# Sliding-window attention followed by a hard-swish MLP on one core: batch 0's values loaded by heads, and batch 1's attention moved against its MLP units

## The chip, the cores and the metric

The kernel runs on one core of a Trainium2 chip. A core has five engines that run their own instruction streams in order and meet at semaphores: TensorE (matmuls and transposes, into PSUM), VectorE, ScalarE, GpSimd (called POOL in the profile) and SyncE (SP), which here only issues DMAs. The metric is device time in microseconds (us), the median of several executions.

## The reference

Inputs are q, k, v of shape (8 batches, 8 heads, 576 tokens, 64), and two weights, w_in (512 x 2048) and w_out (2048 x 512). All are float32.

```python
scores = q @ k.T / 8            # per batch and head
scores = where(0 <= i - j < 128, scores - slope[h] * |i - j|, -1e9)
attn = softmax(scores) @ v      # causal, a window of 128 tokens
x = attn laid out as (8 * 576 tokens, 512)
h = x @ w_in                    # 512 -> 2048
g = h * clip(h + 3, 0, 6) / 6
out = g @ w_out                 # 2048 -> 512, 4608 rows
```

## The kernel before

**Attention, by pairs of heads.** The unit of attention is a pair g = 4b + hp: batch b, heads 2hp and 2hp+1. There are 32 pairs. q and k are cast to bf16 and transposed on TensorE into `qTb` and `kTb` (one copy each for even and odd batches). `double` (line 248) transposes two pairs of one of q and k in two parts through a small PSUM bank, `wide_double` (276) all of it through a wide score buffer. `scores_diag` (313) and `scores_off` (341) make the scores of the diagonal and the off-diagonal blocks in two score buffers of tag "sc", of which there are two in all. `exp_diag` and `exp_off_full` (371, 362) take the exponentials on ScalarE into `pd` and `po`; for batch 1, GpSimd masks the diagonal blocks. `attend` (434) and `attend_split` (444) multiply by the values `vbuf`, which carry a column of ones for the sums, and VectorE divides (a reciprocal and a product) into `avs`. `back` (462) transposes `avs` into `xT`, the MLP's input, five transposes on TensorE and a copy out of PSUM.

**MLP, by tiles and units.** The 4608 rows are cut into nine tiles of 512. A tile has 16 up units (`moe_up`, 508): four matmuls of 128x512 over the model dimension, then ScalarE's relu (516), then VectorE's product (517) into `gbuf`. It has 16 down units (`moe_down`, 534): four matmuls each into one row block of 128. `up_begin` and `up_more` (496, 501) issue some of an up unit's matmuls ahead. `ORDER` (559) is a string of U and D per tile that fixes the order of units; `fill(n)` (569) issues the next n of them, and goes no further than the batches whose attention is finished (`done`).

**PSUM.** Banks are shared by tag: "sc" two wide buffers, "h" two, "av" one, "o" one. An instruction that first writes a bank waits until the last reader of its former contents is done. `UP_BANKS` (506) tells which of the first tile's up units use "av" or "o" instead of "h".

**Order.** The program is scheduled by hand: each engine gets its instructions in the order in which the Python code writes them, and nothing is reordered. `first_batch` (604) and `second_batch` (679) write out batches 0 and 1 and the 16 up units of the first tile; `segment` (743) runs the other pairs in a loop. TensorE, ScalarE, VectorE and GpSimd queues, and the DMA queues of SP, ScalarE and GpSimd, are all in that order.

**Loads.** q and k of batch 0 come first, on SP and ScalarE. v of batch 0 comes as five blocks of 128 tokens by all heads (`load_block`, 108), the first quarter of w_in as float32 into half of `gbuf` (`load_raw`, 176; `cast_raw` casts it), the other three quarters by GpSimd's DMA, which casts on the way (`load_w_in`, 168). The exponentials of batch 0 lie in w_out's buffer and those of batch 1 in the second `gbuf`, so w_out is loaded after batch 0. SP's loads of batch 1 (`load_double`, `load_tokens`) come after `attend(0)` in the code.

Of the lines that the steps below speak of, these say most:

```python
UP_BANKS = {2: "av", 5: "o", 8: "av", 11: "o", 12: "av"}            # line 506
eng = nc.vector.tensor_copy if g == 2 * NP - 1 else nc.scalar.copy   # line 478, the copy of back
```

## Time and profile before

| what | value |
|---|---|
| median of 3 runs | 323.69 us (323.47 to 324.67) |
| span of the profiled execution, first to last instruction | 321.8 us |
| the profiled execution's own time | not listed apart from its span; the median lies 1.9 us above the span |
| TensorE busy | 308.2 us, 96% of the span |
| ScalarE, VectorE, GpSimd busy | 196.0, 175.5, 138.4 us |
| granted TensorE clock | 1.00 throughout |
| DMA read and written | 36.70 and 9.44 MB |

The profile is of one execution. A row of a timeline gives the start, the duration, the engine, the line of the kernel, the operation, what it writes and reads, how many instructions are merged in it, and in brackets the engine's idle time before it and who ended it. A row's duration is from its first start to its last end; back to back, the next one starts a little earlier than that end. A row of windows gives each engine's busy time and, in parentheses, its number of instructions, and then the clock, the share of the DMA engines that were busy, and GB/s.

### The profile page before, as it was taken

Reading aid. Unit: us, or ns where it says so; the run is one execution under the profiler, and the core shown is the slowest. Engines: PE = TensorE matmul, PEld = TensorE weight load, DVE = VectorE, ACT = ScalarE, POOL = GpSimd, SP = SyncE. Lnnn points to the kernel's source line nnn. Section 1 sums busy time; section 2 is a strip of 40 time slices with the busy share of each in tenths; the row PEclk is TensorE's granted clock in tenths of the full one; section 3 lists DMA queues with packets and bytes.
Section 4 is the critical chain, followed back from the end, with each engine's and each line's share of the span. In section 5 each row is a group of like instructions: output and inputs, shape, how many; then the busy total and the mean of one; then the engine's idle time right before and its main releaser. Section 6 shows DMA issues by size and latency. Waiting matters only on the chain.

```text
span 321.8 us, 6865 instructions
## 1 busy us (share of the span) xinstructions
PE 308.2 (96%) x2620; PEld 164.6 (51%) x2659; DVE 175.5 (55%) x346; ACT 196.0 (61%) x337; POOL 138.4 (43%) x247
## 2 busy tenths in 40 slices
PE   6888999999999999999999999999999999999996
PEld 3564465455555545455667655455454444444443
DVE  6686595564346655555555556554655455445510
ACT  3857977877777766766676667666764344244401
POOL 7364590665494767446654663663331000000000
PEclk9999999999999999999999999999999999999999
DMA  7999999899999999999799999922011200000112
GB/s 273 262 369 210 269 233 214 235 200 189 201 256 170 242 200 189 204 202 230 179 214 207 211 189 202 236 66 89 20 55 59 80 34 34 33 33 35 65 49 83
DMA packets 131426, 52.43 MB, mean 163 GB/s; under 512 B 118977, under 2 KB 122817, under 8 KB 131393
## 3 DMA queue, kind: packets, MB, share of 16 engines
q1 hardware_dynamic: 125648, 46.15, 67.0%
q0 software_dynamic: 3696, 3.67, 7.0%
q10 hardware_dynamic: 2048, 2.16, 2.2%
q8 instruction: 21, 0.34, 0.5%
q14 instruction: 13, 0.10, 0.1%
HBM read 36.70 MB, written 9.44 MB: 143 GB/s over the span
## 4 chain that ended last, share of the span: by engine, by line
PE 83%; DMA 7%; ACT 4%; issue 2%; DVE 2%; POOL 1%; SPq 0%; ACTq 0%; DVEq 0%
PE ops L547 37%; PE hps L492 35%; DMA gbuf<-in_moe_w_in_dram 3%; PE scd L324 2%; DMA w_in_sb<-in_moe_w_in_dram 2%; PE av L419 2%; DMA ldbuf<-in_k_dram 2%; PE av L411 2%; ACT r L516 2%; PE sco L356 1%; PE ops L528 1%; DVE gbuf L517 1%; PE tp L254 1%; ACT gbuf L379 1%; ACT xT L479 1%
## 5 line engine op out<-in xcount | busy, mean ns | idle before, releaser
L517 DVE SCALAR_TENSOR_TENSOR gbuf<-r,hps 128x512 bf16<-128x512 f32 x144 | 98.5, 687 | 102.3 <-ACT r L516 99.4
L516 ACT ACTIVATE r<-hps,bias 128x512 f32<-128x512 f32 x144 | 98.8, 690 | 90.4 <-PE hps L492 89.3
L492 PE MATMUL hps<-xT,w_in_sb 128*128 128x512 bf16 (+1 forms) x622 | 143.3, 357 | 2.3 <-DMA w_in_sb<-in_moe_w_in_dram 0.9
L547 PE MATMUL ops<-w_out_sb,gbuf 128*128 128x512 bf16 x539 | 134.0, 379 | 2.4 <-issue 1.7
L492 PEld LDWEIGHTS <-w_in_sb 128*128 128x128 bf16 x640 | 59.0, 98 | 55.3 <-issue 1.7
L547 PEld LDWEIGHTS <-gbuf 128*128 128x128 bf16 x560 | 52.2, 98 | 56.9
L382 POOL TENSOR_SCALAR_AFFINE_SELECT pd<-pd 128x512 bf16<-128x512 bf16 x48 | 29.5, 631 | 37.8 <-ACT pd L379 37.7
L392 POOL TENSOR_SCALAR_AFFINE_SELECT po<-po 128x512 bf16<-128x512 bf16 x48 | 30.1, 633 | 32.6 <-ACT po L389 32.4
L556 DVE COPY osb<-ops 128x512 f32<-128x512 f32 x33 | 22.7, 688 | 22.0 <-PE ops L547 21.9
L379 ACT ACTIVATE pd<-scd,bias_d 128x512 bf16<-128x512 f32 x48 | 31.5, 684 | 4.7 <-PE scd L324 4.7
L389 ACT ACTIVATE po<-sco,bias_o 128x512 bf16<-128x512 f32 x48 | 33.1, 690 | 0.0
L206 POOL CAST tbuf<-ldbuf 128x512 bf16<-128x512 f32 (+1 forms) x45 | 25.5, 611 | 17.1 <-issue 17.1
L430 DVE TENSOR_TENSOR avs<-av,rc 128x384 bf16<-128x384 f32 (+1 forms) x48 | 23.6, 491 | 1.6
L419 PEld LDWEIGHTS <-pd 128*128 128x128 bf16 x192 | 14.3, 97 | 7.9 <-issue 0.5
L411 PE MATMUL av<-vbuf,po 128*128 128x65 bf16 x192 | 18.0, 193 | 0.0
L419 PE MATMUL av<-vbuf,pd 128*128 128x65 bf16 x192 | 17.3, 194 | 0.0
L411 PEld LDWEIGHTS <-po 128*128 128x128 bf16 x192 | 14.3, 98 | 2.9 <-DVE avs L430 0.5
L395 ACT ACTIVATE p4buf<-sco,bias_d 128x64 bf16<-128x64 f32 x48 | 15.6, 325 | 0.0
L199 POOL CAST vbuf<-ldbuf 128x1024 bf16<-128x1024 f32 x14 | 14.2, 1041 | 2.4 <-DMA ldbuf<-in_v_dram 2.4
L324 PEld LDWEIGHTS <-kTb 64*128 64x128 bf16 x256 | 7.3, 94 | 14.3 <-issue 10.0
L324 PE MATMUL scd<-qTb,kTb 64*128 64x128 bf16 x256 | 12.7, 219 | 1.9 <-ACT kTb L232 1.2
L239 POOL CAST pr<-ldbuf 128x576 bf16<-128x576 f32 x18 | 11.5, 671 | 2.0 <-DMA ldbuf<-in_k_dram 1.9
(107 smaller groups left out, 216.7 us busy)
## 6 DMA issues: line engine op xcount, KB each, us to landing
out_dram<-osb SPq DMA_DIRECT2D x33, 256.0 KB, 2.5
ldbuf<-in_v_dram SPq DMA_DIRECT2D x31, 256.0 KB, 5.0
ldbuf<-in_q_dram SPq DMA_DIRECT2D x20, 256.0 KB, 4.8
ldbuf<-in_k_dram SPq DMA_DIRECT2D x16, 256.0 KB, 4.6
ldbuf<-in_q_dram SPq DMA_DIRECT2D x12, 288.0 KB, 6.4
ldbuf<-in_k_dram SPq DMA_DIRECT2D x12, 288.0 KB, 6.7
w_out_sb<-in_moe_w_out_dram POOLq DMA_DIRECT2D x4, 512.0 KB, 10.0
w_in_sb<-in_moe_w_in_dram POOLq DMA_DIRECT2D x3, 512.0 KB, 8.6
```

The lines of the kernel that those rows point to most:

```text
L206: nc.gpsimd.tensor_copy(out=tbuf[:m, :, j, :], in_=s[:m, j, :, :].rearrange("p (i e) d -> p i (e d)", e=2))
L324: nc.tensor.matmul(scd[:, e, ts(j, 128)], lhsT=kT[r, j, :], rhs=qT[r, j, :], start=first, stop=first or j == 3)
L379: nc.scalar.activation(out=pd[:, e, :, :].rearrange("p j c -> p (j c)"), in_=sc[:, e, :], func=ACT.Exp, bias=bias_d[:, h:h + 1], scale=scale)
L382: nc.gpsimd.affine_select(out=pd[:, e, :, :], in_=pd[:, e, :, :], pattern=[[0, 4], [1, 128]], channel_multiplier=-1, base=0, compare_op=AL ...
L389: nc.scalar.activation(out=po[:, e, :, :].rearrange("p j c -> p (j c)"), in_=sc[:, e, :], func=ACT.Exp, bias=bias_o[:, h:h + 1], scale=scale)
L392: nc.gpsimd.affine_select(out=po[:, e, :, :], in_=po[:, e, :, :], pattern=[[0, 4], [-1, 128]], channel_multiplier=1, base=-1, compare_op=A ...
L411: nc.tensor.matmul(out_av, lhsT=po[:, e, qt % 4, :], rhs=vb[:, qt - 1, h, :], start=True, stop=False)
L419: nc.tensor.matmul(out_av, lhsT=d, rhs=vb[:, qt, h, :], start=(qt == 0), stop=True)
L492: nc.tensor.matmul(hps[:, lo:hi], lhsT=w_in_sb[:, ks, ts(ms, 128)], rhs=xT[:, ks, ds(src, hi - lo)], start=(ks == 0), stop=(ks == n_ks - 1))
L516: nc.scalar.activation(out=r6, in_=hps, func=ACT.Relu, bias=bias3[:, 0:1], scale=1.0 / 6.0)
L517: nc.vector.scalar_tensor_tensor(out=gts[nt][:, ms, :], in0=r6, scalar=1.0, in1=hps, op0=ALU.min, op1=ALU.mult)
L547: nc.tensor.matmul(ops[nt, sub], lhsT=gts[nt][:, ms, ts(sub, 128)], rhs=w_out_sb[:, ms, :], start=(ms == 0), stop=(ms == n_ms - 1))
```

## The change

Five things change; no matmul is added or taken away.

- Batch 0's v is loaded by pairs of heads (`load_heads`, the first four token blocks of one head per DMA, and one DMA for the last 64 tokens), all on SP; w_in's first quarter comes in four DMAs between them and is cast on GpSimd alone. `cast_heads` casts v by pairs on GpSimd. Attends 0 and 1 go in between the scores of pairs 2 and 3, and the memsets of `kTb` and `vbuf` for batch 1 stand early now, those of `p4buf` and `tbuf` late.
- SP's loads of batch 1 stand earlier in the code, its v by heads too.
- Up units 0 to 3 are begun before batch 1's first scores, unit 1 in "o" and unit 2 in "av". The wide transposes of batch 1's first half move behind unit 2. The second quarter of w_in is issued between the two halves of batch 1's k cast (`prepare_half`), the third after them.
- In `second_batch`, the transposes of batch 1's second half (now through "av", "o" and "h") and the scores of pairs 4 and 5 come before unit 4; the scores of pairs 6 and 7 among units 4 to 8, and the attends and backs of pairs 4 to 7 among units 8 to 14. Batch 2's double transposes and its first scores come after unit 15. `back` copies with VectorE for all of batch 1.
- The order of the second tile's units begins UUUUD instead of UUDUD.

```diff
--- before.py
+++ after.py
@@ -109,6 +109,12 @@
         n = min(128, S - j * 128)
         eng.dma_start(out=tokens(b, nm)[:n, j, :, :],
                       in_=src_of[nm][b, :, ds(j * 128, n), :].rearrange("h p d -> p h d"))
+
+    def load_heads(b, nm, hp, eng):
+        for e in range(2):
+            h = 2 * hp + e
+            eng.dma_start(out=tokens(b, nm)[:, 0:4, h, :],
+                          in_=src_of[nm][b, h, 0:512, :].rearrange("(j p) d -> p j d", p=128))
 
     def load_tokens(b, nm):
         for j in range(NQ):
@@ -141,12 +147,13 @@
         nc.gpsimd.memset(vbuf[0][:, :, :, D:W], 1.0)
         nc.gpsimd.memset(vbuf[0][64:128, 4, :, 0:D], 0.0)
 
+        nc.gpsimd.memset(kTb[1][:, :, 4, LAST:128], 0.0)
+        nc.gpsimd.memset(vbuf[1][:, :, :, D:W], 1.0)
+        nc.gpsimd.memset(vbuf[1][64:128, 4, :, 0:D], 0.0)
+
     def memsets_later():
         for i in range(2):
             nc.gpsimd.memset(p4buf[i], 1.0)
-        nc.gpsimd.memset(kTb[1][:, :, 4, LAST:128], 0.0)
-        nc.gpsimd.memset(vbuf[1][:, :, :, D:W], 1.0)
-        nc.gpsimd.memset(vbuf[1][64:128, 4, :, 0:D], 0.0)
         nc.gpsimd.memset(tbuf[64:128, :, 4, :], 0.0)
 
     def warm_up(n):
@@ -173,8 +180,8 @@
     raw = gbuf[0][:, n_ms // 2:n_ms, :].rearrange("p m c -> p (m c)").bitcast(FP32).rearrange(
         "p (k f) -> p k f", k=n_ks)
 
-    def load_raw():
-        nc.sync.dma_start(out=raw, in_=moe_w_in[:, 0:512].rearrange("(k p) f -> p k f", p=128))
+    def load_raw(ks):
+        nc.sync.dma_start(out=raw[:, ks, :], in_=moe_w_in[ds(ks * 128, 128), 0:512])
 
     def cast_raw(ks, copy):
         copy(out=w_in_sb[:, ks, 0:512], in_=raw[:, ks, :])
@@ -184,13 +191,12 @@
             out=w_out_sb[:, ts(g, 4), :],
             in_=moe_w_out[ds(g * 512, 512), :].rearrange("(m p) d -> p m d", p=128))
 
-    def second_w_in():
-        nc.gpsimd.memset(w_out_sb[:, 4, 0:1], 0.0)
-        load_w_in(1)
-
     def cast_v(b, j, copy):
         n = min(128, S - j * 128)
         copy(out=vbuf[b % 2][:n, j, :, 0:D], in_=ld[b, "v"][:n, j, :, :])
+
+    def cast_heads(b, hp, copy):
+        copy(out=vbuf[b % 2][:, 0:4, ds(2 * hp, 2), 0:D], in_=ld[b, "v"][:, 0:4, ds(2 * hp, 2), :])
 
     def cast_tokens(b, nm):
         s = ld[b, nm]
@@ -231,6 +237,13 @@
                     nc.tensor.transpose(tp[r, t, :], src[r, ts(t, D)], ident[r, r])
             copy(out=dst[:, hp, :, :].rearrange("p j c -> p (j c)")[:, 0:S].rearrange(
                 "p (a t) -> p a t", t=RT), in_=tp.rearrange("p t a -> p a t"))
+
+    def prepare_half(b, dp, nm, e, copy):
+        if e == 0:
+            st[b, dp, nm] = prs.tile([128, RT, 2 * D], BF16, tag=f"pr{nm}", name="pr2")
+        copy(out=st[b, dp, nm][:, :, ts(e, D)],
+             in_=ldbuf["qk".index(nm)][:, ds((2 * dp + e) * RT * D, RT * D)].rearrange(
+                 "p (t d) -> p t d", t=RT))
 
     def prepare_double(b, dp, copies, nms="kq", early=None):
         for nm, copy in zip(nms, copies):
@@ -459,7 +472,7 @@
     def by_xbar(g):
         return g >= XB and g not in (XB + 2, XB + 3)
 
-    def back(g, tag=None):
+    def back(g, tag=None, place=None):
         b, hp = divmod(g, NP)
         avs = st[g, "avs"].rearrange("p j e d -> p j (e d)")
         if by_xbar(g):
@@ -468,14 +481,16 @@
                 in_=avs.rearrange("p j c -> p (j c)"))
             return
         tag = tag or ("o" if b < 2 else "h")
-        tp = BANKS[tag].tile([128, SP], BF16, tag=tag, name="tb", padded_shape=[128, 1024])
+        tp = place
+        if tp is None:
+            tp = BANKS[tag].tile([128, SP], BF16, tag=tag, name="tb", padded_shape=[128, 1024])
         for j in range(NQ):
             nc.tensor.transpose(tp[:, ts(j, 128)], avs[:, j, :], ident)
         if g == NP - 1:
             nc.scalar.copy(out=xT[:, hp, ds(b % 4 * S, 256)], in_=tp[:, 0:256])
             nc.vector.tensor_copy(out=xT[:, hp, ds(b % 4 * S + 256, S - 256)], in_=tp[:, 256:S])
             return
-        eng = nc.vector.tensor_copy if g == 2 * NP - 1 else nc.scalar.copy
+        eng = nc.vector.tensor_copy if b == 1 else nc.scalar.copy
         eng(out=xT[:, hp, ds(b % 4 * S, S)], in_=tp[:, 0:S])
 
     gts, ops = {}, {}
@@ -493,8 +508,8 @@
                                  rhs=xT[:, ks, ds(src, hi - lo)],
                                  start=(ks == 0), stop=(ks == n_ks - 1))
 
-    def up_begin(nt, ms, n):
-        hps = ps_h.tile([128, NT], FP32, tag="h", name="hps")
+    def up_begin(nt, ms, n, tag="h"):
+        hps = BANKS[tag].tile([128, NT], FP32, tag=tag, name="hps")
         up_mms(nt, ms, 0, n, hps)
         begun[nt, ms] = hps, n
 
@@ -503,7 +518,7 @@
         up_mms(nt, ms, k0, n, hps)
         begun[nt, ms] = hps, n
 
-    UP_BANKS = {2: "av", 5: "o", 8: "av", 11: "o", 12: "av"}
+    UP_BANKS = {5: "o", 8: "av"}
 
     def moe_up(nt, ms):
         gts[nt] = gbuf[nt % 2]
@@ -556,7 +571,7 @@
                 nc.vector.tensor_copy(out=osb, in_=ops[nt, sub])
                 nc.sync.dma_start(out=out[rows, :], in_=osb)
 
-    ORDER = [("UUDUDUUDUUD", "UUDUDUDUD", "UDUDUDD", "UDDDD"),
+    ORDER = [("UUUUDUDUDUD", "UUDUDUDUD", "UDUDUDD", "UDDDD"),
              ("DDDD", "UUDUDUDUD", "UUDUDUDUD", "UUDUDUDDUU"),
              ("DDDD",) * 4]
     units = [(0, moe_up, step) for step in range(16)]
@@ -603,10 +618,15 @@
 
     def first_batch():
         prepare(0, (V, A))
-        load_block(0, "v", 1, nc.scalar)
-        for j in (4, 0, 2, 3):
-            load_block(0, "v", j, nc.sync)
-        load_raw()
+        load_heads(0, "v", 0, nc.sync)
+        load_block(0, "v", 4, nc.sync)
+        load_heads(0, "v", 1, nc.sync)
+        load_heads(0, "v", 2, nc.sync)
+        load_raw(0)
+        load_raw(1)
+        load_heads(0, "v", 3, nc.sync)
+        load_raw(2)
+        load_raw(3)
         warm_up(5)
         tables_diag(0)
         tables_off(0)
@@ -618,6 +638,13 @@
         exp_full(0)
         scores_diag(1)
         prepare_double(0, 1, (V, P), "qk")
+        for dp in range(2):
+            for nm in "kq":
+                load_double(1, dp, nm, nc.sync)
+        load_heads(1, "v", 0, nc.sync)
+        load_block(1, "v", 4, nc.sync)
+        for hp in (1, 2, 3):
+            load_heads(1, "v", hp, nc.sync)
         tables_off(1)
         scores_off(1)
         double_begin(0, 1, "q", ("av", "o"))
@@ -625,115 +652,121 @@
         exp_full(1)
         double_copy(0, 1, "q", 0, (V, V))
         double_copy(0, 1, "k", 0, (A, A))
+        tables_diag(2)
+        tables_off(2)
         scores_diag(2)
         double_copy(0, 1, "q", 1, (V, V))
         double_copy(0, 1, "k", 1, (V, V))
-        tables_off(2)
         scores_off(2)
         exp_full(2)
+        cast_heads(0, 0, P)
+        cast_v(0, 4, P)
+        cast_heads(0, 1, P)
+        cast_heads(0, 2, P)
+        cast_heads(0, 3, P)
+        for ks in range(n_ks):
+            cast_raw(ks, P)
+        attend_split(0, ("av", "o"))
         scores_diag(3)
-        cast_v(0, 4, P)
-        cast_v(0, 0, P)
-        cast_v(0, 1, P)
-        cast_v(0, 2, V)
-        cast_v(0, 3, V)
+        attend_split(1, ("h", "h"))
         scores_off(3)
         exp_full(3)
-        attend(0)
-        for dp in range(2):
-            for nm in "kq":
-                load_double(1, dp, nm, nc.sync)
-        load_tokens(1, "v")
-        attend_split(1, ("av", "h"))
         attend(2)
-        back(0, "o")
-        cast_raw(0, P)
-        cast_raw(1, P)
+        back(0, "av")
+        back(1, "o")
         attend(3)
-        cast_raw(2, A)
-        back(1, "av")
-        cast_raw(3, P)
-        prepare_double(1, 0, (P,), "k")
-        second_w_in()
-        up_begin(0, 0, 1)
-        up_begin(0, 1, 1)
-        back(2, "o")
+        back(2, "h")
+        up_begin(0, 0, 2)
+        back(3, "av")
+        up_begin(0, 1, 2, "o")
+        up_more(0, 0, 3)
+        up_more(0, 1, 3)
+        prepare_half(1, 0, "k", 0, P)
+        load_w_in(1)
+        prepare_half(1, 0, "k", 1, P)
+        load_w_in(2)
         prepare_double(1, 0, (V,), "q")
-        up_more(0, 0, 2)
-        up_more(0, 1, 2)
-        back(3, "av")
+        up_more(0, 0, 4)
+        up_more(0, 1, 4)
+        up_begin(0, 2, 4, "av")
+        done[0] = NP
+
+    def second_batch():
+        g = NP
         wide_double(1, 0, "k", V)
         wide_double(1, 0, "q", A)
-        up_more(0, 0, 3)
-        up_more(0, 1, 3)
-        done[0] = NP
+        up_begin(0, 3, 4)
+        fill(1)
+        prepare_double(1, 1, (P,), "k")
+        load_w_in(3)
+        prepare_double(1, 1, (P,), "q")
+        scores_diag(g)
+        exp_diag(g, 0)
+        exp_diag(g, 1)
+        fill(1)
+        scores_off(g)
+        exp_off_full(g)
         fill(2)
-        prepare_double(1, 1, (P,), "k")
-        load_w_in(2)
-        prepare_double(1, 1, (P,), "q")
-        load_w_in(3)
+        double(1, 1, "k", 0, "av", V)
+        double(1, 1, "k", 1, "o", V)
+        scores_diag(g + 1)
+        exp_diag(g + 1, 0)
+        exp_diag(g + 1, 1)
+        double(1, 1, "q", 0, "h", A)
+        double(1, 1, "q", 1, "h", V)
         for dp in range(2):
             for nm in "kq":
                 load_double(2, dp, nm, nc.sync)
-
-    def second_batch():
-        scores_diag(NP + 0)
-        exp_diag(NP + 0, 0)
-        exp_diag(NP + 0, 1)
-        fill(2)
-        scores_off(NP + 0)
-        exp_off_full(NP + 0)
-        wide_double(1, 1, "k", V)
-        fill(1)
-        wide_double(1, 1, "q", V)
-        fill(1)
-        scores_diag(NP + 1)
-        exp_diag(NP + 1, 0)
-        exp_diag(NP + 1, 1)
-        fill(2)
-        scores_off(NP + 1)
-        exp_off_full(NP + 1)
-        fill(1)
-        cast_tokens(1, "v")
-        scores_diag(NP + 2)
-        exp_diag(NP + 2, 0)
-        exp_diag(NP + 2, 1)
-        fill(1)
-        scores_off(NP + 2)
-        exp_off_full(NP + 2)
-        fill(2)
-        for i in range(0, 4):
+        scores_off(g + 1)
+        exp_off_full(g + 1)
+        memsets_later()
+        fill(1)
+        cast_heads(1, 0, P)
+        cast_v(1, 4, P)
+        scores_diag(g + 2)
+        exp_diag(g + 2, 0)
+        exp_diag(g + 2, 1)
+        fill(1)
+        scores_off(g + 2)
+        exp_off_full(g + 2)
+        fill(1)
+        cast_heads(1, 1, P)
+        scores_diag(g + 3)
+        exp_diag(g + 3, 0)
+        exp_diag(g + 3, 1)
+        fill(1)
+        scores_off(g + 3)
+        exp_off_full(g + 3)
+        fill(1)
+        attend(g)
+        fill(1)
+        cast_heads(1, 2, P)
+        attend(g + 1)
+        back(g, "o")
+        fill(1)
+        cast_heads(1, 3, P)
+        for i in range(4):
             load_w_out(i)
-        g = 2 * NP - 1
-        scores(g)
-        exp_diag(g, 0)
-        exp_diag(g, 1)
-        prepare_double(2, 0, (V, P))
-        prepare_double(2, 1, (P, P))
+        prepare_double(2, 0, (P, P), "kq")
+        back(g + 1, "o")
+        attend(g + 2)
+        fill(1)
+        attend(g + 3)
+        prepare_double(2, 1, (P, P), "kq")
         nc.gpsimd.memset(ldbuf[2][:, 0:1], 0.0)
         load_tokens(2, "v")
         for dp in range(2):
             load_double(3, dp, "k", nc.sync)
         load_tokens(3, "q")
-        exp_off_full(g)
-        fill(1)
-        attend(NP)
-        fill(1)
-        attend(NP + 1)
-        fill(1)
-        back(NP)
-        attend(NP + 2)
-        fill(1)
-        back(NP + 1)
+        fill(1)
+        back(g + 2, "o")
+        fill(1)
+        back(g + 3, "o")
+        fill(2)
+        done[0] = 2 * NP
         double(2, 0, "k", 0, "av", A)
-        attend(NP + 3)
-        back(NP + 2)
         double(2, 0, "k", 1, "av", A)
         wide_double(2, 0, "q", A)
-        up_begin(1, 0, 3)
-        back(2 * NP - 1)
-        up_begin(1, 1, 3)
-        done[0] = 2 * NP
         fill(2)
         scores_diag(2 * NP)
         scores_off(2 * NP)
@@ -796,10 +829,8 @@
         load_double(0, 1, "q", nc.sync)
         constants()
         memsets()
-        memsets_later()
         first_batch()
         second_batch()
-        fill(2)
         segment(2 * NP, G, lambda g: FILLS.get(g, (1, 1, 1, 2, 0, 1, 2)))
         done[0] = G
         fill(len(units))
```

## The prediction

> **What bounds the kernel now.** I read the page's first two parts, then the table of ten-microsecond windows, then the timelines of TensorE, ScalarE and VectorE up to 56 us, and last the DMA issues and rates up to 60 us.
>
> ```profile
> span 321.8 us, 6865 instructions
> PE 308.2 (96%) x2620; PEld 164.6 (51%) x2659; DVE 175.5 (55%) x346; ACT 196.0 (61%) x337; POOL 138.4 (43%) x247
> ```
>
> TensorE is busy for 308.2 of 321.8 us. The change takes no matmul away, so all it can move is TensorE's 13.6 us of idle time. The windows say where that lies.
>
> ```profile
> 0.00:10.00 10.00, 7.11 (x112) 3.70 (x113) 7.16 (x34) 4.84 (x6) 7.01 (x22) 1.00 0.87 268
> 10.00:20.00 10.00, 9.13 (x166) 6.31 (x164) 6.64 (x18) 7.71 (x11) 3.23 (x6) 1.00 1.19 315
> 20.00:30.00 10.00, 7.72 (x76) 4.37 (x77) 7.85 (x12) 7.07 (x11) 8.07 (x14) 1.00 1.20 270
> 30.00:40.00 10.00, 9.95 (x91) 4.88 (x92) 5.67 (x9) 8.73 (x14) 4.25 (x6) 1.00 1.16 251
> 40.00:50.00 10.00, 9.30 (x137) 6.38 (x139) 8.78 (x16) 8.25 (x14) 8.63 (x15) 1.00 1.09 232
> ```
>
> The columns are PE, PEld, DVE, ACT, POOL, then clock, DMA share and rate. TensorE idles 2.9, 0.9, 2.3, 0.05 and 0.7 us: 6.8 us up to 50 us, of which 1.43 us is the start. From 30 us on TensorE is full, ScalarE at 8.73 and VectorE at 8.78 are close behind it, and this is the stretch that the change reorders most.
>
> ```profile
> 7.31 0.40 PE L324 MATMUL scd<-qTb,kTb 64*128 64x128 bf16 x8 [1.15 <-ACT kTb L232]
> 21.69 0.45 PE L473 MATMUL tb<-ident,avs 128*128 128x128 bf16 x5 [0.39 <-DVE avs L441]
> 24.90 0.40 PE L324 MATMUL scd<-qTb,kTb 64*128 64x128 bf16 x8 [0.34 <-ACT qTb L284]
> 29.52 1.04 PE L492 MATMUL hps<-xT,w_in_sb 128*128 128x512 bf16 x3 [0.90 <-DMA w_in_sb<-in_moe_w_in_dram]
> ```
>
> The first four attends' divisions on VectorE run one after another until 21.6 us and hold the last transposes back. The scores of pair 4 wait for ScalarE's copy of q, and the fifth up unit waits 0.9 us for w_in's second quarter. That last wait is what the change aims at.
>
> ```profile
> 23.73 1.12 ACT L284 COPY qTb<-tp 128x1152 bf16<-128x1152 bf16 x1 [1.17 <-PE tp L282]
> 24.74 1.27 ACT L516 ACTIVATE r<-hps,bias 128x512 f32<-128x512 f32 x2
> 25.90 1.28 ACT L379 ACTIVATE gbuf<-scd,bias_d 128x512 bf16<-128x512 f32 x2
> 27.04 1.29 ACT L516 ACTIVATE r<-hps,bias 128x512 f32<-128x512 f32 x2
> 28.18 1.07 ACT L363 ACTIVATE gbuf<-sco 128x1024 bf16<-128x1024 f32 x1
> ```
>
> Back to back, a relu or half a diagonal exp holds ScalarE 0.58 us, a wide exp 0.93 (34.89 to 35.86, 41.49 to 42.39), a q copy 1.01. This queue begins at 23.73, once batch 1's q has landed (issued from 14.60, median 6.4 us: about 21.7), has been cast (0.74) and transposed (0.5).
>
> ```profile
> 43.13 0.69 DVE L517 SCALAR_TENSOR_TENSOR gbuf<-r,hps 128x512 bf16<-128x512 f32 x1 [0.64 <-ACT r L516]
> 43.73 0.21 DVE L440 RECIPROCAL rcw<-wide 128x10 f32<-128x10 f32 x1
> 43.98 0.82 DVE L441 TENSOR_TENSOR avs<-wide,rcw 128x640 bf16<-128x640 f32 x1
> 44.72 0.68 DVE L517 SCALAR_TENSOR_TENSOR gbuf<-r,hps 128x512 bf16<-128x512 f32 x1
> ```
>
> On VectorE an up unit holds 0.60 us, an attend 0.99, a transposed copy about 0.38 (0.46 in the trace).
>
> **The change, part by part.**
>
> Start. The v load on ScalarE's queue goes; it stands at 6.18 for 0.39 us ahead of the kTb copy that the 1.15 us wait is for. The copy can start at 6.2 instead of 6.62: batch 0 runs 0.4 us earlier to about 12 us. The memsets taken from POOL there (0.69 us) have no waiter.
>
> Batch 0. Attends 0 and 1 go in between the scores, on v that arrives by head pairs. Pair 0 is two DMAs of 128 KB. A v block's 256 KB move in about 1.25 us (the rate of 195 to 223 GB/s in the three slices after 9 us), so half takes 0.62; pairs land at about 11.2, 13.0, 14.2 and 17, and POOL casts each in 0.61. Seven DMAs more on SP (nine for five, four for one) at 0.6 us of issue each lie beside transfers of equal length, so the bytes ahead of batch 1's q, and its landing, stay: at best 1 us earlier, at worst 1 us later, taken as nothing. With two attends done by 15.4, the last back transposes run at 19.6, not 21.7, and ups 0, 1, 2 are issued by 22.0. Casting w_in's first quarter on POOL alone ends near 19.9, k's first half near 20.5, so the second quarter is issued at 20.5 instead of 21.98 and lands (7.5 us, from the chain of waits: 21.98 to 29.47) near 28.
>
> Where TensorE's lead ends. The k transposes wait for POOL's second half (22.0), those of q for VectorE (22.8): ScalarE's q copy starts at 23.5, 0.2 us earlier than before. Up 3 and the scores of pair 4 follow, and TensorE has finished at 25.9 what it had finished at 27.94: a lead of 2.0 us. Next it must transpose k of pairs 6, 7 into the one "av" bank, which holds up unit 2. That frees when VectorE has used unit 2's relu, and ScalarE comes to it after q copy, relu 0, two diagonal exps, relu 1, wide exp: 23.5 + 1.0 + 0.58 + 1.14 + 0.58 + 0.93 = 27.75; relu 0.69 and product 0.69 give 29.2. **TensorE stands 3.3 us**, with scores 5, its exps, the remaining doubles and all ups queued behind it. In the meantime the w_in wait of 0.9 us is gone: w_in has landed by then.
>
> From 29.2 to 41. The scores of pair 5 start at 29.7, so ScalarE, too, has stood 1.2 us. The first exps of pair 5, then the q copy (0.65) release the "h" bank for up 4 at 32.1 (TensorE waits 0.7). From there ScalarE is full: three more wide exps, two more pairs of diagonal exps, relus 4 to 7, and relu 8 begins at 39.6, product 8 at 40.4. TensorE, held two score banks ahead at most, has attend 5 done at 40.8.
>
> From 41 to the second batch's end. The four backs are now VectorE copies (three were ScalarE's), each through the one "o" bank, while batch 2's double k, its wide q and the first ups of the next tile stand behind the last back instead of between the attends. VectorE's queue from 40.4 to back 7's copy is six products, four attends, three copies = 3.6 + 4.0 + 1.1 = 8.7 us, with 0.2 and 0.5 us in which relus 10 and 11 are late: back 7's transposes can run at 49.4. TensorE's waits on the way, laid out instruction by instruction: back 4 waits for avs 4 (1.3), back 5 for the "o" copy (0.8), back 7 the same (1.1). Then ups 14, 15 (1.7 us) and the double k into "av" twice, where the second waits for ScalarE's copy behind relus 14 and 15 (1.3). Two first-tile ups later the scores of pair 8 start at 55.4; before, at 51.58.
>
> Sum: lead −2.0; waits after it 3.3 + 0.7 + 1.3 + 0.8 + 1.1 + 1.3 = 8.5 against 2.5 before (27.94 to 51.58 is 23.6 us for 21.1 us of TensorE work): −2.0 + 6.0 = +4.0. The new order of units UUUU for UUDU puts an up where a down stood: up 2 of tile 1 waits about 0.4 us for an "h" bank; I set that off against the 0.5 us of idle that TensorE had from 50 to 70 and may give back. POOL's casts of values, the w_out issues (at 40.1 instead of 40.73) and SP's loads of batch 2 lie ahead of their users by 3 us or more and cost nothing; should v of batch 1 land 3 us later than its 39, attend 7 would be late next. Span 321.8 + 4.0 = 325.8; 1.9 us lies between that span and the median 323.69, kept: **327.6 us**.
>
> Bounds: if only the waits that one bank forces (3.3, 0.7, 1.3) stay and the other three shrink to nothing, −2.0 + 5.3 − 2.5 = +0.8, 324.5. If all stay and q lands 1 us late, +5, 328.7. I take the full list, since VectorE's chain alone gives 49.4. The likeliest case's own range is 325.3 to 329.5.
>
> **The rivals.**
>
> Not slower: TensorE keeps its lead. Place: the "av" transposes after the scores of pair 4. If unit 2's product is done by 26 instead of 29.2, the waits of 3.3 and 0.7 go and ScalarE stays ahead: doubles 1.0, scores 3.6 and ups 4 to 8 4.3 end at 34.8, product 8 starts at 35.7, and VectorE's chain of 9.0 us (40.4 to 49.4) and the 6.0 from there to pair 8 give 50.7 against 51.58: 322.8. For it speaks that ScalarE stands idle from 20.4 to 23.5; against it that relu 0 is written behind the q copy. Only with the tail's waits gone too (−2.0 and 1.5 us less idle than before) would it be 320.2, clearly faster.
>
> Half the loss, and the same within 0.5% (1.6 us, about what a measurement of this kernel can tell from no change): the 3.3 us wait is real but VectorE's tail fills as well as before, the lower bound above, 324.5. For it: in the trace, VectorE was as loaded from 43 to 49.6 and TensorE lost only 0.7. Against it: then transposes and ups filled the gaps; now they stand behind.
>
> Slower by the clock: a hole of 3.3 us, three times the longest now (1.15). The five warm-up matmuls took 2.31 us where later four of the same size take 0.86, about double. [...]
>
> Slower by the loads: SP issues 16 pieces in place of nine ahead of batch 1's second half; if q lands 2 us later, everything from 23.5 does: 329.6. Against it: four v issues in a row (4.67 to 9.86) kept the transfers dense. [...]
>
> **How the numbers follow.** Forecast 0.51, clock 0.09, loads 0.07: slower by over 0.5% is 0.67. The two cases near the time before, 0.09 each, make same 0.18; both halves going at once is what is left, faster 0.15. The range from 322.3 to 330.0 takes in both near cases and both slower rivals and leaves the faster one out.
>
> **What would show it.** In the changed kernel: a TensorE wait of about 3 us near 26 at the double transposes (line 254 of the kernel before), released by VectorE's product; ScalarE without gaps from 32 to 41; waits of about 1 us at the back transposes of batch 1, released by VectorE; no wait for w_in; the first scores of batch 2 near 55. I am wrong if the double transposes at 26 wait under 1 us, or if the scores of pair 8 start before 52.

## The result: 3.1% slower, 2.6 times the loss that was forecast

| | before | after |
|---|---|---|
| median | 323.8 us (323.47 to 324.67) | 334.04 us (333.36 to 334.86) |
| ratio | | 1.0311, 95% interval 1.0285 to 1.0337 |
| span of the profiled execution | 321.8 us | 332.7 us (its own time 334.49) |
| TensorE busy, idle | 308.2, 13.6 us | 310.9, 21.8 us |

The forecast was 327.6 us with a range to 330.0. Slower was right; but the loss is 10.2 us where 3.9 were forecast, and the time lies outside the range. The page of the changed kernel begins so (span, then busy time, share and number of instructions by engine):

```profile
span 332.7 us, 6885 instructions
PE 310.9 (93%) x2621; PEld 166.7 (50%) x2659; DVE 175.0 (53%) x348; ACT 195.0 (59%) x334; POOL 141.4 (42%) x253
```

Of 10.9 us of span, 8.2 are new idle time and 2.7 are the same matmuls taking longer. The ten-microsecond windows of the changed kernel say where (PE, PEld, DVE, ACT, POOL, then the granted clock, DMA share, GB/s):

```profile
10.00:20.00 10.00, 9.24 (x171) 6.62 (x169) 7.53 (x20) 8.23 (x11) 5.32 (x9) 1.00 0.99 212
20.00:30.00 10.00, 6.17 (x58) 3.42 (x60) 4.81 (x7) 5.13 (x9) 8.00 (x13) 1.00 1.14 312
30.00:40.00 10.00, 8.68 (x73) 4.93 (x73) 4.62 (x7) 6.76 (x11) 4.99 (x10) 0.66 1.11 206
40.00:50.00 10.00, 8.31 (x116) 5.29 (x118) 6.92 (x14) 5.71 (x10) 8.56 (x15) 1.00 1.03 267
50.00:60.00 10.00, 7.91 (x84) 4.58 (x82) 5.50 (x11) 6.66 (x10) 1.86 (x5) 1.00 1.19 202
...
80.00:90.00 10.00, 8.83 (x85) 4.63 (x85) 4.70 (x10) 7.27 (x15) 4.05 (x9) 1.00 1.15 226
```

Before, the last of these windows was

```profile
80.00:90.00 10.00, 9.83 (x90) 5.18 (x90) 4.08 (x9) 7.38 (x15) 4.98 (x9) 1.00 1.14 210
```

Three things are to be seen that the forecast did not have. The loads run at 212 GB/s from 10 to 20 us where they ran at 315 (four kernels below, which are the same up to there, show 218 to 264). The granted clock is 0.66 from 30 to 40 us, where it was 1.00. And TensorE idles as late as 80 to 90 us (8.83 busy against 9.83), long after the part of the code that the forecast followed.

TensorE's timeline of the changed kernel, rows with the waits in brackets:

```profile
23.96 1.39 PE L295 MATMUL tp<-ident,pr 128*128 128x128 bf16 x18 [0.87 <-POOL pr L244]
...
26.56 0.40 PE L337 MATMUL scd<-qTb,kTb 64*128 64x128 bf16 x8 [0.34 <-ACT qTb L297]
...
31.10 1.12 PE L267 MATMUL tp<-ident,pr 128*128 128x128 bf16 x9 [3.27 <-DVE gbuf L532]
...
46.06 0.45 PE L488 MATMUL tb<-ident,avs 128*128 128x128 bf16 x5 [0.85 <-DVE avs L454]
48.00 0.44 PE L488 MATMUL tb<-ident,avs 128*128 128x128 bf16 x5 [0.63 <-DVE xT L494]
53.30 0.44 PE L488 MATMUL tb<-ident,avs 128*128 128x128 bf16 x5 [0.90 <-DVE xT L494]
56.88 0.38 PE L267 MATMUL tp<-ident,pr 128*128 128x128 bf16 x4 [1.14 <-ACT kTb L269]
59.43 0.40 PE L337 MATMUL scd<-qTb,kTb 64*128 64x128 bf16 x8
...
62.97 1.02 PE L507 MATMUL hps<-xT,w_in_sb 128*128 128x512 bf16 x4 [1.27 <-DVE gbuf L532]
...
83.23 1.02 PE L562 MATMUL ops<-w_out_sb,gbuf 128*128 128x512 bf16 x4 [0.95 <-DVE osb L571]
```

The big wait is where it was forecast, in size (3.27 for 3.3) and releaser (the product that empties "av"), and so are the four waits of the tail, the stretch of batch 1's attends and backs (46.06 to 56.88). The wait for w_in is gone. The last two waits, of 1.27 and 0.95 us, were not forecast. ScalarE's queue shows the chain behind the big wait as it was written down: q copy, relu, exps, relu, wide exp, and only then unit 2's relu, the first in the last row.

```profile
25.39 1.12 ACT L297 COPY qTb<-tp 128x1152 bf16<-128x1152 bf16 x1 [4.16 <-PE tp L295]
26.40 0.69 ACT L531 ACTIVATE r<-hps,bias 128x512 f32<-128x512 f32 x1
27.00 1.26 ACT L392 ACTIVATE gbuf<-scd,bias_d 128x512 bf16<-128x512 f32 x2
28.15 0.69 ACT L531 ACTIVATE r<-hps,bias 128x512 f32<-128x512 f32 x1
28.72 1.03 ACT L376 ACTIVATE gbuf<-sco 128x1024 bf16<-128x1024 f32 x1
29.62 1.28 ACT L531 ACTIVATE r<-hps,bias 128x512 f32<-128x512 f32 x2
```

But the q copy starts at 25.39 and not at 23.5. VectorE's timeline says why: VectorE stood ready and waited for the load. Before, the cast began at 21.55, the second row.

```profile
23.17 1.45 DVE L252 CAST pr<-ldbuf 128x576 bf16<-128x576 f32 x2 [1.59 <-DMA ldbuf<-in_q_dram]
21.55 1.40 DVE L239 CAST pr<-ldbuf 128x576 bf16<-128x576 f32 x2
```

The second of the two loads of q landed at 23.84 us, and at 21.99 before. This place moves from one execution to the next. In the profiles of four kernels below that are the same up to here, that load lands at 22.96 to 23.77 and the q copy starts at 24.51 to 25.32.

Three landmarks split the miss of this execution. The end of pair 4's scores was forecast at 25.9 and came at 27.83: +1.9 (in the four other profiles 26.95 to 27.77, so +1.0 to +1.9). From there to pair 8's first scores 29.5 us were forecast (to 55.4) and 31.6 were taken (to 59.43): +2.1. From pair 8 to the end 270.4 were forecast, 273.3 were taken: +2.9. Together 6.9, the distance of the measured span from the forecast one (332.7 and 325.8); the median misses by 6.4, since the profiled execution is one of the longer ones.

### The profile page after: what moved, and what is told of

Same layout as the page of the kernel before. It is cut to its first block, busy times and chain, and to the rows that moved or that the text cites. A ratio compares the mean times of both kernels' runs of the same rounds, so it can differ in the third digit from the quotient of the medians.

```text
span 332.7 us, 6885 instructions
## 1 busy us (share of the span) xinstructions
PE 310.9 (93%) x2621; PEld 166.7 (50%) x2659; DVE 175.0 (53%) x348; ACT 195.0 (59%) x334; POOL 141.4 (42%) x253
## 4 chain that ended last, share of the span: by engine, by line
PE 80%; ACT 5%; DMA 5%; DVE 4%; issue 3%; SPq 1%; POOL 1%; ACTq 0%; POOLq 0%; DVEq 0%
PE ops L562 35%; PE hps L507 34%; PE scd L337 2%; ACT r L531 2%; PE av L432 2%; DMA ldbuf<-in_k_dram 2%; PE av L424 2%; DVE gbuf L532 1%; PE tp L267 1%; PE sco L369 1%; DMA xT<-avs 1%; DMA ldbuf<-in_v_dram 1%; PE ops L543 1%; ACT gbuf L392 1%; SPq L116 1%
## 5 line engine op out<-in xcount | busy, mean ns | idle before, releaser
L337 PEld LDWEIGHTS <-kTb 64*128 64x128 bf16 x256 | 7.5, 96 | 13.5 <-issue 10.3
L205 POOL CAST vbuf<-ldbuf 128x1024 bf16<-128x1024 f32 x12 | 12.1, 1041 | 0.0
```

Of the source, the lines that this page charges most:

```text
L337: nc.tensor.matmul(scd[:, e, ts(j, 128)], lhsT=kT[r, j, :], rhs=qT[r, j, :], start=first, stop=first or j == 3)
```

## The experiments

Except where noted each starts from the changed kernel. All times stand beside the kernel before at 323.75 to 324.0 us in the same sittings, and ratios are to it.

**Batch 0 as before, everything else changed.** The old v blocks, casts and places of the attends, w_in's first quarter in one transfer:

```diff
-        load_heads(0, "v", 0, nc.sync)
...
-        load_raw(3)
+        load_block(0, "v", 1, nc.scalar)
+        for j in (4, 0, 2, 3):
+            load_block(0, "v", j, nc.sync)
+        load_raw_whole()
...
-        attend_split(0, ("av", "o"))
...
+        attend(0)
```

> The changed kernel, with batch 0 as it was before: v by blocks of tokens (block 1 on ScalarE's queue), w_in's first quarter in one DMA and cast as before, attends 0 and 1 behind the scores of pair 3. All from unit 0 on stays changed. Theory of the loads: with v by heads, batch 1's first q lands at 23.84 us instead of about 22.0, and everything from ScalarE's q copy (25.39) on is late by that; so this run should bring the q copy back to about 23.5 and be 1.5 to 2.2 us faster than the changed kernel (334.0): about 332. Theory of the order: what is lost is lost behind the q copy, and batch 0's attends in their old place take away TensorE's lead of 2 us, which was the good part: 334 to 336.

Measured: 333.86 us, ratio 1.0300 (1.0281 to 1.0320), the same as the changed kernel. The hole of 3.27 us is there at 28.68. So q's later landing in the changed kernel is not, by itself, what the loss hangs on. With the old batch 0 the second load of q lands at 21.72 us and no longer at 23.84, but batch 0 ends later: VectorE comes to the q cast only at 23.60, behind the copies of the last back, and the q copy starts at 26.23.

**Batch 0 as changed, everything else before.** The counterpart:

```diff
 # before.py
-        load_block(0, "v", 1, nc.scalar)
-        for j in (4, 0, 2, 3):
-            load_block(0, "v", j, nc.sync)
-        load_raw()
+        load_heads(0, "v", 0, nc.sync)
+        load_block(0, "v", 4, nc.sync)
...
+        load_raw(3)
...
```

> The complement: the kernel before, with only batch 0 changed (v by heads, w_in's first quarter in four pieces, attends 0 and 1 between the scores; the memsets exchanged); the up units, batch 1 and the order of units as before. Theory of the loads: q lands near 23.8 here too, ScalarE's queue starts 1.5 to 1.9 us late, 325.0 to 326.0 against 323.8. Theory that batch 0's part is a gain by itself: TensorE is 2 us ahead at the last back transposes and keeps it, 321.5 to 322.5.

Measured: 325.5 us, 1.0044 (1.0026 to 1.0062). TensorE's timeline of this kernel shows what it costs alone: batch 0 is done early, and then the transposes of k and q wait.

```profile
23.96 0.68 PE L295 MATMUL tp<-ident,pr 128*128 128x128 bf16 x9 [2.66 <-POOL pr L252]
25.52 1.14 PE L295 MATMUL tp<-ident,pr 128*128 128x128 bf16 x9 [0.89 <-DVE pr L252]
```

The lead is real, but what is to use it is not there yet: the front half of the change buys time that batch 1's loads, later than before, do not let it spend.

**The same, with w_in's first quarter in one transfer.** This asks which of the smaller pieces delays q:

```diff
-        load_raw(0)
-        load_raw(1)
         load_heads(0, "v", 3, nc.sync)
-        load_raw(2)
-        load_raw(3)
+        load_raw_whole()
```

> The kernel before with the new batch 0 (as in the run that changed batch 0 alone, 325.5), but w_in's first quarter in one DMA behind v's last heads, as before; v stays by heads. Theory of the pieces of w_in: batch 1's first q lands near 22 instead of 24.7 and the waits of 2.7 and 0.9 us at 21 to 25 us shrink to under 1: 323.0 to 324.0. Theory of the pieces of v: nine half-size loads, eight of which may be under way, leave the DMA engines short from 9 to 15 us; q lands at 23.5 to 24.5 again: 325 to 326.

Measured: 325.22 us, 1.0033 (1.0019 to 1.0048); the intervals overlap. In the profiles the second load of q lands at 24.69 us with four pieces and at 22.90 with one, between the two expectations. The DMA rates in slices of 1.5 us from the start, the kernel with four pieces first:

```profile
GB/s 0 147 409 375 390 344 224 149 131 187 248 320 272 346 393 407 361 236 183 192 211 201 198 196 197 261 271 359 392 373 172 198 165 164 205 205 201 194 248 246
```

and with one transfer:

```profile
GB/s 0 134 393 401 409 343 215 206 174 123 325 386 384 373 403 382 259 209 202 223 197 202 192 201 263 267 353 394 372 170 194 160 161 206 205 204 193 250 239 191
```

Both kinds of piece go with a lower rate. While the v pieces of 128 KB move it falls to 131 and 123 GB/s at the lowest, where blocks of 256 KB held 195 to 223 before. The four slices with the w_in pieces (13.5 to 19.5 us) show 187 to 320, those with the one transfer (15 to 21 us) 325 to 386; the last v pieces run among the w_in pieces, so the two are not told apart there. The time hardly follows. The likely reason is that w_in's own cast is then late (TensorE waits 1.4 us for `w_in_sb` from GpSimd, 1.3 for the second quarter); no run separates it.

**The hole filled.** Fourteen matmuls into an "h" bank that nobody reads, behind pair 4's scores; nothing of the work is left out:

```diff
+    def keep_busy(n):
+        w2 = ps_h.tile([128, 4, 128], FP32, tag="h", name="w2")
+        rhs = ident.rearrange("p (j c) -> p j c", j=1).to_broadcast([128, 4, 128])
+        for _ in range(n):
+            nc.tensor.matmul(w2, lhsT=ident, rhs=rhs, start=True, stop=True)
...
         exp_off_full(g)
+        keep_busy(14)
```

> The changed kernel with 14 matmuls of 128x512 without use put into TensorE's wait of 3.27 us (after the scores of pair 4, into the free h bank, 3.0 us of work), so that the wait stays as long but the array doesn't stand. Theory of the clock: the changed kernel's granted clock is 0.66 in the window from 30 to 40 us because TensorE stood, and its matmuls there take double; this run shows 1.00 there and is 1.5 to 2.5 us faster: 331.5 to 332.5. Rival: from 30 to 40 ScalarE sets the pace and slow matmuls hide behind it: no change, 333.5 to 334.5.

Measured: 332.32 us, 1.0258 (1.0228 to 1.0288), 1.7 less than the changed kernel. Its window and the rows around the filled hole:

```profile
30.00:40.00 10.00, 9.71 (x107) 5.24 (x106) 5.36 (x8) 8.77 (x15) 5.87 (x12) 1.00 1.03 204
```

```profile
27.80 3.18 PE L169 MATMUL w<-ident 128*128 128x512 bf16 x14
31.04 0.66 PE L273 MATMUL tp<-ident,pr 128*128 128x128 bf16 x9
31.63 0.40 PE L343 MATMUL scd<-qTb,kTb 64*128 64x128 bf16 x8
```

The transposes start at the same time as with the hole (31.04 for 31.10), yet take 0.66 us and not 1.12. From the end of pair 4's scores to pair 8's first scores this kernel takes 29.4 us (27.77 to 57.15) and the changed one 31.6. The clock's loss is a cost of its own, apart from the wait.

**The hole half filled.** Six matmuls instead of fourteen:

```diff
-        keep_busy(14)
+        keep_busy(6)
```

> The changed kernel with six matmuls of 128 x 512 whose result nobody reads, in the bank "h", behind the scores of pair 4: about 1.3 us of the 3.3 us in which TensorE stands are filled, a hole of about 2 us stays. If the clock falls only after one unbroken hole of more than 3 us, the granted clock from 30 to 40 us is 0.9 or more and the time is that of the kernel with the hole filled whole, 332.3 us. If holes that lie close together add up (with the one of 0.87 us before them), the clock from 30 to 40 us is still near 0.67 and the time is 333.5 to 334.2 us.

Measured: 331.86 us, 1.0248 (1.0213 to 1.0282), the clock 1.00 from 30 to 40 us. A hole of 1.77 us is left, which in this profile does not drop the clock:

```profile
30.51 0.66 PE L273 MATMUL tp<-ident,pr 128*128 128x128 bf16 x9 [1.77 <-DVE gbuf L538]
```

Of the four executions one, at 333.11 us, has a mean clock of 0.995 over its span, where the others have 0.999 to 1.00, so there it did fall somewhere. The stretch between the two landmarks takes 29.4 us again (27.24 to 56.60). The gain of 2.2 us is not shown to differ from the 1.7 of the full filling.

**The up units' products ahead of the wide copies.** Units 0 to 2 get their relus and products written ahead of batch 1's first q and k copies, so that "av" comes free early:

```diff
-        prepare_double(1, 0, (V,), "q")
...
+        fill(3)
+        prepare_double(1, 0, (V,), "q")
...
-        fill(2)
+        fill(1)
```

> The changed kernel with units 0, 1 and 2's relus and products put ahead of the wide copies of batch 1's first k and q on ScalarE and VectorE (ScalarE stands idle for 4.16 us there). Theory of the order: the av bank that holds unit 2 is then free when TensorE has issued pair 4's scores; the wait of 3.27 us goes or falls under 0.5, the clock stays 1.00 for lack of a long wait, and ScalarE gets its exps 1.7 us earlier: 328 to 330.5. Rival: the time is set further on, by VectorE's queue of products, divisions and back copies, and the start only lengthens the waits there: 333 to 334.

Measured: 332.48 us, 1.0263 (1.0227 to 1.0300). The hole of 3.27 shrinks to 1.37, and 2.75 us of waiting appear one step earlier: the q cast now stands behind the products in VectorE's queue. The wait moved along the queue more than it went away. The profile is of the slowest of the four executions (333.82 us), and its clock fell elsewhere, behind a wait in batch 0 (the last section).

**The tail as before.** Units between attends 4 and 5 and back 4, batch 2's double k and the ups of the next tile between the backs, copies of backs 4 to 6 on ScalarE:

```diff
-        eng = nc.vector.tensor_copy if b == 1 else nc.scalar.copy
+        eng = nc.vector.tensor_copy if g == 2 * NP - 1 else nc.scalar.copy
...
+        back(g + 1, "o")
+        double(2, 0, "k", 0, "av", A)
+        fill(1)
...
```

> The changed kernel with the stretch behind the scores of pair 7 laid out as before: an up unit between attends 4 and 5 and back 4, batch 2's double k and the first matmuls of the next tile's units 0 and 1 between the attends and backs, and three of the four backs copied by ScalarE again. Theory of the tail: of the TensorE waits at back 4, back 5, back 7 and the second double k (0.85, 0.63, 0.90, 1.14 us, 3.5 in all) one at most is left; 2.0 to 3.0 us faster than the changed kernel (334.0): 331 to 332. Rival: VectorE's queue of products and divisions sets the time there whatever stands between: 333.5 to 334.5.

Measured: 331.09 us, 1.0207 (1.0181 to 1.0233), 2.95 less. TensorE's timeline of this kernel has none of the four tail waits left, and pair 8's scores stand at 55.30:

```profile
55.30 0.40 PE L337 MATMUL scd<-qTb,kTb 64*128 64x128 bf16 x8
56.72 1.02 PE L507 MATMUL hps<-xT,w_in_sb 128*128 128x512 bf16 x4 [0.41 <-DVE gbuf L532]
59.24 1.02 PE L507 MATMUL hps<-xT,w_in_sb 128*128 128x512 bf16 x4 [1.27 <-DVE gbuf L532]
```

Not all of the 4.1 us by which these come earlier is the tail's: the clock was low for 3.4 us in this execution and for 6.8 in the changed kernel's. From there to the end of its span of 328.7 us it takes 273.4, as the changed kernel does (273.3). The wait of 1.27 after pair 8 is not of the tail.

**The units as before.** The other half of what happens after pair 8: the old string in `ORDER`, and the `fill(2)` that stood between `second_batch` and the loop:

```diff
-    ORDER = [("UUUUDUDUDUD", "UUDUDUDUD", "UDUDUDD", "UDDDD"),
+    ORDER = [("UUDUDUUDUUD", "UUDUDUDUD", "UDUDUDD", "UDDDD"),
...
         second_batch()
+        fill(2)
         segment(2 * NP, G, lambda g: FILLS.get(g, (1, 1, 1, 2, 0, 1, 2)))
```

> The changed kernel with the second tile's units in the order of before (UUDUD) and with the two units issued before pair 9's stage, as before; the change had taken both out, so that the loop over the pairs starts two units behind. Theory of the units: the loss after pair 8's scores (they start 7.9 us later than before, the end comes 10.6 us later) is due to that: the waits of 1.27 us at 61.7 and 0.95 us at 82.3 go, 1.5 to 2.7 us faster than the changed kernel: 331.3 to 332.5. Rival: units only move and TensorE's work is the same: 333.5 to 334.5.

Measured: 331.31 us, 1.0208 (1.0178 to 1.0238), 2.7 less. In its timeline the waits of 1.27 and 0.95 are gone and the tail's stay:

```profile
54.97 0.38 PE L267 MATMUL tp<-ident,pr 128*128 128x128 bf16 x4 [1.14 <-ACT kTb L269]
57.52 0.40 PE L337 MATMUL scd<-qTb,kTb 64*128 64x128 bf16 x8
```

From 57.52 to the end of its span (328.2) are 270.7 us; before it was 270.2 (51.58 to 321.8). So of the 2.9 us after pair 8, 2.6 are the units'. Other profiles bear this out: from pair 8 to the end the kernels with the new units take 272.8 to 273.4 us, those with the old ones, here and in the two experiments that follow, 270.6 to 270.7. That pair 8 itself comes 1.9 us earlier here is not the edit's, which changes only what follows: in this execution q landed earlier and the clock was low for 3.4 us. The string and the missing `fill(2)` were not tried apart.

**Products, tail and units put back together.** The three edits above in one kernel, the products this time behind the q cast.

> The changed kernel with three things at once: units 0 to 2's relus and products ahead of the wide copies (but behind VectorE's cast of q), the tail of before, and the units' order of before. Theory that the loss is the sum of the waits that these three make (3.3 with a clock loss of 1.7, 2.5, 2): 7 to 8 us faster than the changed kernel, 326 to 327.5, with the 1.5 us of batch 0's loads left. Rival: a limit that stands behind them all, ScalarE's or VectorE's queue, keeps half of it: 329 to 331.

Measured: 326.92 us, 1.0087 (1.0058 to 1.0115), 7.1 less than the changed kernel, where the three alone gave 1.6, 2.95 and 2.7, together 7.25. They add up within the intervals, each of about 1 us either way. 2.9 us are left by the median, but the clock has a part in them: three of the six executions have a mean clock of 0.999 to 1.00 and take 325.65 to 326.35 us, three have 0.989 to 0.994 and take 327.49 to 328.08. The profile is of the slowest; it has two holes between 22.9 and 28.4:

```profile
24.24 1.39 PE L295 MATMUL tp<-ident,pr 128*128 128x128 bf16 x18 [1.30 <-POOL pr L244]
25.47 1.03 PE L507 MATMUL hps<-xT,w_in_sb 128*128 128x512 bf16 x4
28.32 0.40 PE L337 MATMUL scd<-qTb,kTb 64*128 64x128 bf16 x8 [1.82 <-DVE kTb L297]
```

**And batch 0 too.** Batch 0 as in the first experiment besides, so that of the change only batch 1's middle is left (the "rope products" of the expectation are the up units' products):

> The changed kernel with four of its parts put back as they were: batch 0 (v in blocks, w_in's first quarter in one transfer, the old casts and the old order of pairs), the rope products ahead of the wide copies, the tail, and the order of units with its fill(2). What is left of the change is batch 1's middle: transposes and scores of pairs 4 and 5 ahead of unit 4, w_in's second quarter issued between, v by heads in batch 1. If the parts found so far are the whole loss (batch 0 alone 1.5 us, tail 2.95, units 2.7, clock 1.7, order of the products the rest), this gives 324.0 to 325.5 us and a granted clock of at least 0.9 between 30 and 40 us. If the middle itself costs something, the time stays at that of the kernel with three parts undone, 326 to 327.5, with a hole of 1.5 us or more on TensorE between 22 and 32 us.

Measured: 326.39 us, 1.0065 (1.0040 to 1.0089), the second of the two expectations. The middle alone costs about 2 us, with two holes of 1.36 and 1.38 us in TensorE's timeline; the w_in wait of 0.9 that they replace is gone:

```profile
27.76 0.40 PE L340 MATMUL scd<-qTb,kTb 64*128 64x128 bf16 x8 [1.36 <-DVE kTb L300]
...
31.73 0.38 PE L270 MATMUL tp<-ident,pr 128*128 128x128 bf16 x4 [1.38 <-DVE gbuf L535]
```

**Batch 1's v by heads alone**, in the kernel before:

```diff
 # before.py
-        load_tokens(1, "v")
+        load_heads(1, "v", 0, nc.sync)
+        load_block(1, "v", 4, nc.sync)
+        for hp in (1, 2, 3):
+            load_heads(1, "v", hp, nc.sync)
...
-        cast_tokens(1, "v")
+        cast_heads(1, 0, P)
+        cast_v(1, 4, P)
...
```

> The kernel before with one part of the change: batch 1's v is loaded by heads (nine transfers in place of two) and cast to bfloat16 pair by pair in GpSimd's queue, everything else in the old order. The kernel with all but batch 1's middle put back measured 326.4 us, 2.4 above before. If these 2.4 us are the order of transposes, scores and units in the middle, this kernel gives 323.6 to 324.5 us, no change. If they are batch 1's values by heads (the loads' rate, or casts that come late for the products), it gives 325.5 to 327 us and a wait of TensorE for vbuf or for GpSimd near 45 to 60 us.

Measured: 324.85 us, 1.0018 (1.0004 to 1.0032): some 0.6 us, between the two expectations.

**Two units ahead instead of three**, in the kernel that has only the middle left:

```diff
-        up_begin(0, 2, 4, "av")
...
-        fill(3)
...
-        up_begin(0, 3, 4)
+        fill(2)
...
         exp_diag(g, 1)
+        fill(2)
         scores_off(g)
```

> The kernel with all but batch 1's middle put back (326.4 us), with one more edit: only two units, as in the kernel before, stand ahead of batch 1's first transposes, their products come behind the copies of kT and qT, and units 2 and 3 stand between the two kinds of scores of pair 4. If the 1.8 us that the middle's order costs beyond v by heads (0.6) come from the third unit and its products ahead of the copies (kT's copy at 26.35 us against 23.10 before, holes of TensorE of 1.36 and 1.38 us behind it), the time falls to 324.3 to 325.2 us and the kT copy is back before 24 us. If they come from pair 5's transposes in halves and the later part of the middle, the time stays at 326 to 327 us.

Measured: 325.57 us, 1.0070 (1.0044 to 1.0096). The copy of kT begins at 24.09 and no longer at 26.35, about where the first theory put it, but the ratio is that of the kernel with three units (1.0065). The third unit shows no cost; the intervals leave room for about 1 us.

**The q cast first** on VectorE's queue, and its transposes ahead of the last parts of units 0 and 1, on top of the last kernel:

```diff
         up_begin(0, 0, 2)
+        prepare_double(1, 0, (V,), "q")
         back(3, "av")
...
+        wide_double(1, 0, "k", V)
+        wide_double(1, 0, "q", A)
         up_more(0, 0, 4)
...
```

> The kernel with two units ahead (325.6 us, 1.8 above before), with one more edit: batch 1's first q cast stands ahead of the copies of back 3 on VectorE, and its transposes ahead of the last parts of units 0 and 1 on TensorE, both as in the kernel before. There the q cast began at 21.55 us and the scores of pair 4 at 24.90; with two units ahead the cast began at 22.77, 1.2 later, behind the copies, and the scores at 26.11, 1.2 later too. If that place in VectorE's queue is what is left of the middle, the scores begin by 25.2 us and the time is 324.2 to 325.0, v by heads alone (324.6 to 324.9). If not, the time stays at 325.4 to 326.2 although the scores begin earlier.

Measured: 325.18 us, 1.0040 (1.0026 to 1.0053). Pair 4's scores come at 25.75, 0.36 sooner than in the last kernel and still 0.85 later than before:

```profile
25.75 0.40 PE L340 MATMUL scd<-qTb,kTb 64*128 64x128 bf16 x8 [0.78 <-ACT qTb L300]
26.08 1.90 PE L510 MATMUL hps<-xT,w_in_sb 128*128 128x512 bf16 x8
```

The ratio falls by 0.3%, with intervals that just overlap, so the q cast's place may be a part of the 2 us, and v by heads another. The places in single profiles say little here: those scores come at 25.36 and 25.73 in the profiles of two kernels with the old batch 0 (w_in earlier, and batch 1's v by heads). Neither, nor both, is shown to be the whole.

**w_in earlier, nothing else**, in the kernel before: the attempt to have the gain that the change was after without its cost.

```diff
 # before.py
         cast_raw(3, P)
+        load_w_in(1)
         prepare_double(1, 0, (P,), "k")
-        second_w_in()
```

> The kernel before with one edit: w_in's second quarter is issued ahead of batch 1's k cast on GpSimd's queue and not behind it. It would take the wait for w_in at 28.6 us (0.9 us) away and hand over the k transposes a little later. If that wait is on the path: 323.0 to 323.5 us against 324.0. If the k and q loads share their rate with the 1 MB of w_in, the q transposes come later by as much and the time is the same or up to 1 us more: 324.0 to 325.0. Nothing of the kernel's work is left out.

Measured: 323.94 us, 0.9994 (0.9978 to 1.0009). The wait for w_in falls from 0.9 to 0.3 us, and nothing is gained that can be measured. Where the 0.6 us go is not shown. In the profile pair 4's scores come 0.46 us later than before, which may be the price that the second expectation names or the spread between executions. No kernel tried here beats the one before.

## Why the prediction was right in direction and short by 6.4 us

- *"TensorE stands 3.3 us"*: right, 3.27, with the order on ScalarE that it was worked out from. The mechanism of the wait was understood; what went wrong lies before it, in its consequence, and after it.
- *"so the bytes ahead of batch 1's q, and its landing, stay ... taken as nothing"*: this step failed. The bytes stayed; the rate did not (212 GB/s from 10 to 20 us, 315 before). The second load of q landed at 23.84 instead of 21.99, the q copy began at 25.39 instead of the 23.5 forecast, and the lead of 2.0 us at the end of pair 4's scores was 0.1 (27.83 for 27.94). That is the first 1.9 us, of an execution at the upper end of 1.0 to 1.9. The rival by the loads had the place right and the price nearly, and was given 0.07 on the ground that four v issues in a row had kept the transfers dense; those were of 256 KB. The experiments add a limit: batch 0 by heads costs 1.5 us in the kernel before, but with the old batch 0 the changed kernel is no faster, since then batch 0's own end is later.
- *"Slower by the clock"*, a rival at 0.09: it happened, beside the forecast and not instead of it. This step failed too. The granted clock is 0.50 from 30.4 to 37.3 us, and from pair 4's scores to pair 8's the changed kernel takes 31.6 us. Both kernels with the hole filled take 29.4, the 29.5 of the forecast, and so the +2.1 is the clock's. In the medians the filling gave back 1.7 and 2.2. The mistake was to hold the rival for another course of events, when the forecast's own 3.3 us hole was its cause: with the hole filled, wholly or by half, the clock is 1.00 from 30 to 40 us. No trace of the kernel before, whose clock is 1.00 throughout, shows the cost with which the range to 330.0 takes in this rival; the runs showed stretches of 3.4 or 6.8 us at 0.50, in the changed kernel 6.8. ScalarE, too, did as forecast only with the hole filled: from 32 to 41 us it was busy for 8.9 and 9.0 of 9 us there and for 6.9 in the changed kernel, where TensorE at half clock held it back.
- *Waits of 1.3, 0.8, 1.1 and 1.3 us in the tail*: all four came, as 0.85, 0.63, 0.90 and 1.14. 4.5 was forecast, 3.5 measured, and the tail put back gave 2.95. The 0.7 for "h" was 0.22. All waits of the stretch come to 7.2 and not 8.5. That its 29.5 us held in the filled kernels is in part luck: the 21.1 us of TensorE's work were too few, since its busy time there before is 21.9 by the windows, and the two errors nearly cancel. The tail's own sum does not close either: 40.4 + 8.7 + 0.2 + 0.5 is 49.8, not 49.4.
- *"The new order of units ... I set that off against the 0.5 us of idle"*: this step failed, and is the largest. The term was put at nothing and measured 2.6 us by the traces (273.3 to 270.7 from pair 8 to the end) and 2.7 by putting the units back. It looked at the string and missed the last edit of the diff, which the list of the change leaves out as well: the `fill(2)` between `second_batch` and the loop is gone, so the loop starts two units behind. Two new waits, 1.27 us at 62.97 for a product and 0.95 at 83.23 for an output copy, come with the new units and go with them; which of the two edits makes them is open.
- *Start 0.4 us earlier*: right in some executions. The copy of kT that was to move is at 6.64 in the changed kernel's profile, before at 6.62, because its transposes ended no earlier; in the profiles of two kernels with the same start (batch 0 as changed, tail as before) it is at 6.24 and 6.23, near the 6.2 forecast.
- *The w_in wait of 0.9 us is gone*: right, but an edit that shortens this wait alone gained nothing (0.9994).

So the sum, 4.0 forecast and 10.9 measured in spans: 1.9 from a term set to nothing, 2.1 from a rival that was no rival, 2.9 after pair 8, of which 2.6 are the units and 0.2 the forecast's own rounding (its 55.4 for pair 8 is 3.8 us and not 4.0 behind 51.58). What stays open: some of the 2 us that batch 1's middle costs alone, and the split between the string of units and the two units that are missing.

## What to carry to other kernels

Read the diff's last hunk with the care of its first: an order written out by hand is a budget, and a call that drops out of a balance (here two units) shifts everything behind it. A hole that the forecast itself predicts has its consequences inside the forecast: ask what a hole of that length does to the clock (here 6.8 us at 0.50 after 3.27 us) before calling that a rival. And before moving work to remove a wait, try the smallest edit that shortens it: if that gains nothing, as here, what the rest of the change costs is likely to be pure loss.
